# A channel-attention kernel on one core: the last row of two transfers sent in 16 narrow blocks

## The chip, the core and the metric

The kernel runs on one core of a Trainium2 chip. A core has five engines with a queue of instructions each: PE (TensorE, matrix products), DVE (VectorE), ACT (ScalarE), POOL (GpSimd) and SP (SyncE, which here does nothing but issue transfers). Transfers between the chip's memory (HBM) and the core's own memory (SBUF, 128 partitions) are carried out by 16 transfer engines, which the profile calls DMA engines. The metric is the time of one execution on the device in microseconds (us). Lower is better.

## The reference

```python
x: (1, 384, 384, 384) bfloat16      # batch, height, width, channels
g = einsum("bhwc->bc", x) / (H * W) # mean of each channel
s = sigmoid(g * w1d[0])             # k = 1: one weight, no neighbours
return x * s[:, None, None, :]
```

So there are 147,456 rows of 384 channels (768 bytes each). All of them have to be read before the first one can be scaled, and all of them are written.

## The kernel before

**Two passes.** The rows are spread over the 128 partitions, 1152 rows a partition. Pass one loads every row and adds it up; pass two multiplies every row by `s` and stores it. The SBUF tile `arena` has 275 rows a partition, far fewer than 1152, so pass one keeps only a part: 71 rows as they are, and 296 more packed four into three (`fold`, line 292, moves bits of every fourth row into spare bits of the other three; `unfold`, line 470, takes them out again). The other 785 rows of a partition are "streamed": they are read in pass one, summed and overwritten, and read a second time in pass two. That gives the 190.41 MB read and 113.25 MB written of the profile.

**The sum.** `sum_rows` (line 253) adds a row with one matmul against a tile of ones, into the PSUM tile `bank0`; each matmul (line 242) waits for the load of its row. `take_raw` (line 433) loads rows that stay as they are and sums them; the loop in line 437 ends pass one with slots of 13 rows and then V (8 rows), Y (8), T (5) and T+5 (3 rows). T and Y are scratch of `fold` and can be loaded only when the last `fold` is through. When the last row is summed, ACT computes the sigmoid (line 443) and copies it (line 447); then the scaling (line 456, mostly on DVE) and the stores (line 466) begin.

**Pass two** is laid out in advance by a small planner in Python (from line 564): it keeps a model time, decides which rows are scaled, unpacked, stored or loaded next, and so fixes the order of the instructions of each queue. It uses a cost for a row (`ROW`), for a load and for a store; nothing of it runs on the chip. The last store that it plans holds 15 rows a partition.

**Waits.** `Flow` (line 21) records every step with what it reads and writes. `Flow.emit` (line 68) turns the dependences into semaphore waits. Of a step's waits, all but one are put into the queue as wait instructions ahead of it (line 112), the last one rides on the instruction itself (line 117); the waits are sorted so that the latest step comes first (line 79). All loads and stores are issued by SP. The transfers use 24 semaphores in turn ("lanes", line 26), so a transfer also waits for the one 24 places before it. At the end SP waits for the last transfer of each lane (lines 123 and 124), in the order in which the lanes were first used.

Of the kernel before, what the change touches and what calls it, by code (L numbers as in the profile page):

```python
# [20 lines left out]
class Flow:  # L21
# [46 lines left out]
    def emit(self):  # L68
        nc = self.nc
        engines = {"SP": nc.sync, "ACT": nc.scalar, "PE": nc.tensor, "DVE": nc.vector, "POOL": nc.gpsimd}  # L70

        know = {e: {} for e in engines}

        def covers(k, d):
            return k.get(d.lane, 0) >= d.rank if d.dma else k.get(d.eng, -1) >= d.i

        for s in self.steps:
            k = know[s.eng]
            for d in sorted(s.deps, key=lambda d: -d.i):
                if covers(k, d):  # L80
                    continue
                s.waits.append(d)
                d.wanted = True
                for key, v in d.know.items():
                    if k.get(key, -1) < v:
                        k[key] = v
            s.know = dict(k)
            if s.dma:
                s.know[s.lane] = s.rank
            else:  # L90
                s.know[s.eng] = s.i

        count, sems = {}, {}
        for s in self.steps:
            if not s.dma and s.wanted:
                s.rank = count[s.eng] = count.get(s.eng, 0) + 1

        def sem(s):
            key = s.lane if s.dma else s.eng
            if key not in sems:  # L100
                name = f"f_{key[0]}{key[1]}" if s.dma else f"f_{key}"
                sems[key] = self.tc.alloc_semaphore(name)
            return sems[key]

        last = {}
        with self.tc.tile_critical():  # L106
            for s in self.steps:
                eng = engines[s.eng]
                waits = [(sem(d), d.rank * (16 if d.dma else 1)) for d in s.waits]
                hold = None if s.dma or not waits else waits.pop()  # L110
                for h, v in waits:
                    eng.wait_ge(h, v)  # L112
                ins = s.emit()
                if ins is None:
                    continue
                if hold:
                    ins = ins._wait_ge(*hold)
                if s.dma:
                    ins.then_inc(sem(s), 16)
                    last[s.lane] = s  # L120
                elif s.wanted:
                    ins.then_inc(sem(s), 1)
            for lane, s in last.items():
                engines[lane[0]].wait_ge(sem(s), 16 * s.rank)
# [3 lines left out]
def kernel(  # L128
# [11 lines left out]
    nc = tc.nc  # L140
    P = nc.NUM_PARTITIONS
# [4 lines left out]
    RPP = HW // P  # L146
# [15 lines left out]
    T = A + N_A  # L162
# [20 lines left out]
    ones = pool.tile([P, P], bf16, name="ones")  # L183
# [4 lines left out]
    arena = pool.tile([P, ROWS, C], bf16, name="arena")  # L188
# [10 lines left out]
    xf = x.rearrange("b h w c -> (b h w) c")  # L199
    of = out.rearrange("b h w c -> (b h w) c")  # L200

    def view(t, r0, n):
        return t[r0 * P : (r0 + n) * P, :].rearrange("(p r) c -> p r c", r=n)

    def rows(lo, n):
        return [("a", r) for r in range(lo, lo + n)]
# [17 lines left out]
    def raw(a):  # L224

        return c_raw + (a - U if a < G0 else PAIR + a - V)


    summed = [0]

    def load(chunk, a, lo, hi):

        r0, n = chunk
        fl.add(
            "SP",
            lambda: nc.sync.dma_start(out=arena[:, a : a + hi - lo, :], in_=view(xf, r0, n)[:, lo:hi, :]),  # L236
            writes=rows(a, hi - lo), dma=True,
        )
# [14 lines left out]
    def sum_rows(a, n):  # L253
        def emit(i, first, last):
            if first:
                return nc.tensor.matmul(acc, lhsT=ones[:], rhs=arena[:, i, :], start=first, stop=last)  # L256
            return add_held(arena[:, i, :], last)

        for i in range(a, a + n):
            first, last = summed[0] == 0, summed[0] == RPP - 1  # L260
            fl.add(
                "PE", lambda i=i, f=first, l=last: emit(i, f, l),
                reads=[("a", i), "ones"], writes=["bank0"],
            )
            summed[0] += 1

# [163 lines left out]
            stream_all(where[1])  # L430
    assert streamed[0] == N_STREAM

    def take_raw(a, n):
        load(KEPT, a, raw(a), raw(a) + n)
        sum_rows(a, n)

    for a, n in S2 + [(U, 8)] + S3 + S1 + [(V, 8), (Y, 8), (T, 5), (T + 5, 3)]:
        take_raw(a, n)
    assert summed[0] == RPP

    fl.add(
# [9 lines left out]
    def scale(a, n, eng="DVE", s=s_bf, after=()):  # L451
# [7 lines left out]
            reads=rows(a, n) + ["s_bf" if s is s_bf else "bank0"], writes=rows(a, n), after=after,  # L459
        )  # L460

    def store(chunk, a, lo, hi):
        r0, n = chunk
        return fl.add(
            "SP",
            lambda: nc.sync.dma_start(out=view(of, r0, n)[:, lo:hi, :], in_=arena[:, a : a + hi - lo, :]),
            reads=rows(a, hi - lo), dma=True,
        )
# [219 lines left out]
    while True:  # L688

        if dve_at <= now:  # L690
            ahead = backlog()
            can = bool(turns)
            if not can and not alongside and (ahead >= PENDING or not landed):
                can = start_group()
            if landed and (ahead < PENDING or not can):
                chunk, a, lo, n, end = landed.popleft()
                scale(a, n, s=s_ps if alongside and now else s_bf)
                dve_at = now + TT(n)
                since = (a, lo) if since is None else since
                if end or ahead < MERGE:  # L700
                    b, first = since
                    send(chunk, b, first, lo + n, stored(b, lo + n - first))
                    since = None
            elif can:
                f, t, then = turns.popleft()
                f()
                dve_at = now + t
                if then:
                    then()
        if alongside and alongside[0][0] <= now:  # L710
            _, chunk, a, lo, n = alongside.popleft()
            store(chunk, a, lo, lo + n)
            moves.append([now + LAT, n * ROW + PER_STORE, stored(a, n)])
        while waiting and waiting[0][0] <= now:
            _, n, then, chunk, a, lo, known = waiting.popleft()
            known.append(store(chunk, a, lo, lo + n))
            moves.append([now + LAT, n * ROW + PER_STORE, then])
        if not asked and not line and not turns:
            verdict()
            asked = True  # L720
        if out_rows == total and not checked:
            checked = True
            fl.add("POOL", again, reads=["odd_i", "s_bf"], writes=rows(Y, N_OVER), after=written)
        while over and over[0][0] <= now:
            over.popleft()[1]()

        got = runs()
        if bank_at is None and len(line) <= total - BANKS_AT and got and max(got)[0] >= PS * 4 // 3:
            a = max(got)[1]
            for i in range(a, a + PS * 4 // 3):  # L730
                idle[i] = False
            back = arena[:, a : a + PS, :].rearrange("p r c -> p (r c)")
            for i, bk in enumerate(banks):
                lo, hi = i * BANK, min((i + 1) * BANK, PS * C)
                copy_bank(i, bk[:, 0 : hi - lo], back[:, lo:hi], [("bank", i)], rows(a, PS))
            bank_at = (a, now + 5.0)
            got = runs()

        if got and todo < N_STREAM:
            n, a = max(got)  # L740
            n = min(n, CAP, N_STREAM - todo)
            ahead = backlog()
            if n >= BIG or n == N_STREAM - todo or (ahead < LOW and n >= 8) or ahead < LAST:

                lo = N_STREAM - todo - n
                load(STREAMED, a, lo, lo + n)
                for i in range(a, a + n):
                    idle[i] = False
                parts = [(STREAMED, a + e, lo + e, f - e, f == n) for e, f in split(n, PART)]
                todo += n  # L750
                moves.append([now + LAT, n * ROW + PER_LOAD, lambda parts=parts: landed.extend(parts)])

        if moves and moves[0][0] <= now:
            moves[0][1] -= DT
            if moves[0][1] <= 0:
                over.append((now + SEEN, moves.popleft()[2]))
        else:
            stall += DT
        if not (alongside or moves or waiting or over or landed or line or turns) and todo == N_STREAM:
            break  # L760
        now += DT
    fl.stall, fl.total = stall, now

    nc.scalar.preload_act_table(ACTF.Sigmoid)  # L764
# [31 lines left out]
```

## Time and profile before

| | us |
|---|---|
| median of 3 timed runs | 722.16 |
| lowest and highest | 721.12, 722.69 |
| span of the profiled execution, first to last instruction | 719.6 |
| DVE busy | 494.0 |
| PE busy | 210.5 |
| ACT busy | 115.7 |

A timed run also holds what lies around the span. The profile's page shows 20,160 transfer packets of 303.67 MB on SP's queue. Its views give, for any stretch of the span, the busy time of each engine and the share of the 16 transfer engines that were busy; a share of 0.25 means four of the 16. The chain of waits is the work that ended last, followed back from the end: at each step to what released it. "L242" is line 242 of the kernel; `arena<-in_x_dram` is a load, `out_dram<-arena` a store; `PEld` stands for weight loads and for waits in TensorE's queue, a small `q` for an engine's sequencer (`SPq` issues transfers). The profiler's times are of one execution.

### The profile page before, as it was taken

How to read it: one execution, taken by the hardware profiler on the slowest of the kernel's cores; microseconds unless marked ns; L12 is line 12 of the kernel's file. 1: busy time of each engine (PE TensorE's matmuls, PEld its weight loads, DVE VectorE, ACT ScalarE, POOL GpSimd, SP SyncE). 2: the span in 40 equal slices, each digit the busy share in tenths (PEclk: the TensorE clock that was granted, in tenths of full speed). 3: DMA queues.
4: the chain of work that ended last, by engine and by line, in shares of the span. 5: the costliest groups of instructions: out<-in, count | busy, mean ns of one | idle time of the engine just before them, and what ended most of it. 6: DMA issues, size and time to landing. Idle time of an engine off the chain costs nothing.

```text
span 719.6 us, 2061 instructions
## 1 busy us (share of the span) xinstructions
PE 210.5 (29%) x1202; PEld 0.3 (0%) x3; DVE 494.0 (69%) x471; ACT 115.7 (16%) x93; POOL 10.6 (1%) x7
## 2 busy tenths in 40 slices
PE   4678689888887770000000000000000000000000
PEld 0000000000000000000000000000000000000000
DVE  4600004887999819988999998999998985095500
ACT  3600003665777610002000000000000000000000
POOL 0000000000000005000000000000000000000000
PEclk9999999999999995555555555555555555555555
DMA  9999999999999979999999999999999999999997
GB/s 381 431 441 428 426 430 432 438 434 429 422 427 427 429 324 369 422 394 423 429 432 437 426 431 445 427 428 439 432 427 442 427 436 430 437 435 426 437 438 318
DMA packets 20173, 303.79 MB, mean 422 GB/s; under 512 B 2242, under 2 KB 2242, under 8 KB 6082
## 3 DMA queue, kind: packets, MB, share of 16 engines
q1 hardware_dynamic: 20160, 303.67, 99.0%
q8 instruction: 4, 0.07, 0.0%
q14 instruction: 7, 0.06, 0.0%
q10 hardware_dynamic: 2, 0.00, 0.0%
HBM read 190.41 MB, written 113.25 MB: 422 GB/s over the span
## 4 chain that ended last, share of the span: by engine, by line
DMA 61%; DVE 21%; ACT 6%; PE 5%; another core or an unknown queue 1%; SPq 0%; issue 0%; DVEq 0%
DMA arena<-in_x_dram 40%; DMA out_dram<-arena 21%; DVE arena L456 14%; ACT arena L313 6%; PE bank L242 5%; DVE arena L276 5%; DVE arena L282 2%; SPq L236 0%; ACT s_bf L443 0%; SPq L791 0%; DVEq L112 0%; SPq L106 0%
## 5 line engine op out<-in xcount | busy, mean ns | idle before, releaser
L456 DVE TENSOR_TENSOR arena<-arena,s_bf 128x4608 bf16<-128x4608 bf16 (+8 forms) x97 | 228.8, 2390 | 68.2 <-DMA arena<-in_x_dram 52.3
L276 DVE TENSOR_SCALAR arena<-arena 128x1536 uint16<-128x1536 uint16 (+2 forms) x247 | 145.3, 633 | 111.8 <-DMA arena<-in_x_dram 102.0
L242 PE MATMUL bank<-arena,ones 128*128 128x384 bf16 x1151 | 202.1, 336 | 48.9 <-DMA arena<-in_x_dram 48.9
L313 ACT ACTIVATE arena<-arena 128x3072 uint16<-128x3072 uint16 (+1 forms) x38 | 102.4, 2696 | 142.3 <-DVE arena L276 142.3
L282 DVE TENSOR_TENSOR arena<-arena 128x1536 uint16<-128x1536 uint16 (+2 forms) x114 | 121.0, 1061 | 5.2 <-PE bank L242 2.7
L529 PE MATMUL bank<-odd,ones 128*128 128x1 bf16 x1 | 0.2, 188 | 322.7 <-DVE odd L524 322.7
L456 POOL TENSOR_TENSOR arena<-arena,s_bf 128x1536 bf16<-128x1536 bf16 (+1 forms) x3 | 10.4, 3484 | 268.9 <-ACT bank L447 268.9
L386 ACT COPY arena<-bank 128x512 uint32<-128x512 uint32 (+1 forms) x7 | 4.0, 571 | 58.4 <-DMA out_dram<-arena 58.2
L456 DVE TENSOR_TENSOR arena<-arena,bank 128x1536 bf16<-128x1536 bf16 (+2 forms) x7 | 11.3, 1688 | 0.0
L242 PE MATMUL bank<-zeros,ones 128*128 128x384 bf16 x48 | 8.3, 326 | 0.0
L313 ACT ACTIVATION_READ_ACCUMULATOR arena<-arena 128x1 f32 x38 | 7.1, 186 | 0.0
L386 ACT COPY bank<-arena 128x512 uint32<-128x512 uint32 (+1 forms) x7 | 3.6, 566 | 0.0
L443 ACT ACTIVATE s_bf<-bank,w_sc 128x384 bf16<-128x384 f32 x1 | 0.6, 581 | 14.5 <-PE bank L242 14.5
L256 PE MATMUL bank<-arena,ones 128*128 128x384 bf16 x1 | 0.5, 478 | 6.9 <-DMA arena<-in_x_dram 6.9
L764 ACT ACT_TABLE_LOAD x1 | 1.3, 1283 | 0.7 <-PEq L780 0.7
L343 DVE TENSOR_SCALAR w_sc<-bank 128x1 f32<-128x1 f32 x1 | 0.2, 159 | 1.1 <-PE bank L338 1.1
L333 DVE MEMSET ones<- 128x128 bf16 x1 | 0.2, 165 | 1.0 <-SPq L106 1.0
L338 PE MATMUL bank<-w_bf,ones 1*128 1x1 bf16 x1 | 0.2, 181 | 2.1 <-DMA w_bf<-in_w1d_dram 2.1
L529 PEld LDWEIGHTS bank<-odd,ones 128*128 128x128 bf16 x1 | 0.1, 106 | 581.7 <-DVE odd L524 581.7
L533 DVE CAST odd_i<-bank 128x1 int32<-128x1 f32 x1 | 0.2, 159 | 0.3 <-PE bank L529 0.3
L447 ACT COPY bank<-s_bf 128x192 uint32<-128x192 uint32 x1 | 0.3, 323 | 0.0
L519 DVE TENSOR_REDUCE worst<-seen 128x1 f32<-128x38 f32 x1 | 0.2, 184 | 0.0
(8 smaller groups left out, 0.9 us busy)
## 6 DMA issues: line engine op xcount, KB each, us to landing
arena<-in_x_dram SPq DMA_DIRECT2D x15, 4608.0 KB, 35.4
arena<-in_x_dram SPq DMA_DIRECT2D x21, 1248.0 KB, 13.5
out_dram<-arena SPq DMA_DIRECT2D x7, 3072.0 KB, 33.1
arena<-in_x_dram SPq DMA_DIRECT2D x6, 3072.0 KB, 26.5
out_dram<-arena SPq DMA_DIRECT2D x4, 4608.0 KB, 39.2
arena<-in_x_dram SPq DMA_DIRECT2D x6, 2304.0 KB, 18.2
arena<-in_x_dram SPq DMA_DIRECT2D x3, 4512.0 KB, 27.0
out_dram<-arena SPq DMA_DIRECT2D x10, 1248.0 KB, 12.0
```

Of the source, the lines that this page charges most:

```text
L242: return pe.add_instruction(mybir.InstMatmult(name=nc.get_next_instruction_name(), ins=[pe.lower_ap(rhs), pe.lower_ap(ones[:])], outs=[pe. ...
L256: return nc.tensor.matmul(acc, lhsT=ones[:], rhs=arena[:, i, :], start=first, stop=last)
L276: lambda: nc.vector.tensor_scalar(out=dst, in0=src, scalar1=s0, scalar2=s1, op0=op0, op1=op1),
L282: "DVE", lambda: nc.vector.tensor_tensor(out=dst, in0=a, in1=b, op=op), reads=reads, writes=writes
L313: lambda: nc.scalar.activation(out=y, in_=y, func=ACTF.Copy, accum_out=seen[:, 2 * k + i : 2 * k + i + 1]),
L333: fl.add("DVE", lambda: nc.vector.memset(ones[:], 1.0), writes=["ones"])
L386: "ACT", lambda: nc.scalar.copy(dst.bitcast(u32), src.bitcast(u32)), reads=reads, writes=writes
L443: lambda: nc.scalar.activation(out=s_bf[:], in_=acc, func=ACTF.Sigmoid, scale=w_sc[:, 0:1]),
L447: "ACT", lambda: nc.scalar.copy(s_ps.bitcast(u32), s_bf[:].bitcast(u32)), reads=["s_bf"], writes=["bank0"]
L456: lambda: vec.tensor_tensor(out=v, in0=v, in1=s[:, None, :].to_broadcast([P, n, C]), op=Op.mult),
L529: lambda: nc.tensor.matmul(votes, lhsT=ones[:], rhs=odd[:], start=True, stop=True),
L764: nc.scalar.preload_act_table(ACTF.Sigmoid)
```

## The change

Three things are changed.

- The last load of pass one, three rows a partition to T+5, now loads two rows a partition. The third row (128 partitions x 768 bytes) follows in 16 transfers of 8, 15, 14, ... 2, 1 partitions. They are issued one after the other by SP. The matmuls of T+5 and of the two rows behind it depend on all of them.
- The last store, 15 rows a partition, now stores 14. Its last row is stored in 16 transfers of the same sizes, at the end of SP's queue.
- The closing waits go in the order in which each lane was last used.

All in all SP issues 172 transfers instead of 140, and TensorE's queue has eight more wait instructions, with two semaphores each. The order of instructions on the other engines stays as it is.

```diff
                 if s.dma:
                     ins.then_inc(sem(s), 16)
+                    last.pop(s.lane, None)
                     last[s.lane] = s
...
-    summed = [0]
+    summed, blocked = [0], []
...
-                reads=[("a", i), "ones"], writes=["bank0"],
+                reads=[("a", i), "ones"] + blocked, writes=["bank0"],
...
-    def take_raw(a, n):
-        load(KEPT, a, raw(a), raw(a) + n)
+    BLOCKS = [8] + list(range(15, 0, -1))
+    def take_raw(a, n, blocks=()):
+        r0, m = KEPT
+        load(KEPT, a, raw(a), raw(a) + n - bool(blocks))
+        p, i = 0, raw(a) + n - 1
+        for q in blocks:
+            to, frm = arena[p : p + q, a + n - 1 : a + n, :], view(xf, r0, m)[p : p + q, i : i + 1, :]
+            fl.add("SP", lambda to=to, frm=frm: nc.sync.dma_start(out=to, in_=frm), writes=[("b", a + n - 1, p)], dma=True)
+            blocked.append(("b", a + n - 1, p))
+            p += q
         sum_rows(a, n)
...
-        take_raw(a, n)
+        take_raw(a, n, BLOCKS if a == T + 5 else ())
...
+    n_stored, tails = [0], []
     def store(chunk, a, lo, hi):
         r0, n = chunk
+        n_stored[0] += hi - lo
+        if n_stored[0] == RPP:
+            hi -= 1
+            p = 0
+            for q in BLOCKS:
+                to, frm = view(of, r0, n)[p : p + q, hi : hi + 1, :], arena[p : p + q, a + hi - lo : a + hi - lo + 1, :]
+                tails.append((lambda to=to, frm=frm: nc.sync.dma_start(out=to, in_=frm), rows(a + hi - lo, 1)))
+                p += q
...
+    for f, r in tails:
+        fl.add("SP", f, reads=r, dma=True)
```

More of the change, by code (lines that the diff above doesn't have):

```diff
@@ L431 @@
     assert streamed[0] == N_STREAM
-    def take_raw(a, n):
-        load(KEPT, a, raw(a), raw(a) + n)
+    BLOCKS = [8] + list(range(15, 0, -1))
+    assert sum(BLOCKS) == P
+    def take_raw(a, n, blocks=()):
[7 more added lines that the diff above has]
+            p += q
         sum_rows(a, n)
     for a, n in S2 + [(U, 8)] + S3 + S1 + [(V, 8), (Y, 8), (T, 5), (T + 5, 3)]:
-        take_raw(a, n)
+        take_raw(a, n, BLOCKS if a == T + 5 else ())
     assert summed[0] == RPP
```

## The prediction

> **What bounds the kernel now.** I read the page first (busy times, transfer rates, chain), then the chain near the end of pass one, then busy shares in short windows around the two edited places, then the issues on SyncE's queue.
>
> ```profile
> span 719.6 us, 2061 instructions
> PE 210.5 (29%) x1202; PEld 0.3 (0%) x3; DVE 494.0 (69%) x471; ACT 115.7 (16%) x93; POOL 10.6 (1%) x7
> ...
> q1 hardware_dynamic: 20160, 303.67, 99.0%
> ...
> DMA 61%; DVE 21%; ACT 6%; PE 5%; another core or an unknown queue 1%; SPq 0%; issue 0%; DVEq 0%
> ```
>
> The 16 transfer engines are busy for 99.0% of the span, no compute engine for more than 69%. The bytes stay as they are, so what can move is the time in which the transfer engines are not full. There are two such places, and the change edits both: the turn from pass one to pass two, and the very end. First the chain at the turn (start, us, what), then busy shares in short windows there: the stretch, its length, busy us and count of PE, PEld, DVE, ACT and POOL, the granted clock, the share of the 16 transfer engines, GB/s.
>
> ```profile
> 254.13 11.35 DMA arena<-in_x_dram
> 265.49 0.04 issue
> 265.53 2.77 PE bank L242 x16
> 268.30 0.02 issue
> 268.33 0.59 ACT s_bf L443
> ```
> ```profile
> 264.50:264.90 0.40, 0.40 (x5) 0.00 (x0) 0.00 (x0) 0.00 (x0) 0.00 (x0) 1.00 1.02 411
> ...
> 265.70:266.30 0.60, 0.60 (x5) 0.00 (x0) 0.00 (x0) 0.00 (x0) 0.00 (x0) 1.00 0.32 129
> 266.30:266.70 0.40, 0.40 (x5) 0.00 (x0) 0.00 (x0) 0.00 (x0) 0.00 (x0) 1.00 0.19 75
> 266.70:267.10 0.40, 0.40 (x4) 0.00 (x0) 0.00 (x0) 0.00 (x0) 0.00 (x0) 1.00 0.05 17
> 267.10:270.70 3.60, 1.19 (x8) 0.00 (x0) 1.76 (x3) 0.90 (x2) 1.36 (x1) 1.00 0.00 0
> ```
>
> The engines do not finish together. At 264.9 all are busy, around 266 a share of 0.32 (five of 16), at 267.1 none; then nothing moves until 270.7. But the chain does not run through the last load. It runs through the load of Y (265.49) and the 16 matmuls behind it: eight rows of Y, five of T, three of T+5. The same picture at the end:
>
> ```profile
> 714.00:714.70 0.70, 0.00 (x0) 0.00 (x0) 0.00 (x0) 0.00 (x0) 0.00 (x0) 0.50 0.97 411
> 714.70:715.00 0.30, 0.00 (x0) 0.00 (x0) 0.00 (x0) 0.00 (x0) 0.00 (x0) 0.50 0.55 230
> 715.00:715.50 0.50, 0.00 (x0) 0.00 (x0) 0.00 (x0) 0.00 (x0) 0.00 (x0) 0.50 0.49 207
> 715.50:716.00 0.50, 0.00 (x0) 0.00 (x0) 0.00 (x0) 0.00 (x0) 0.00 (x0) 0.50 0.33 138
> 716.00:717.10 1.10, 0.00 (x0) 0.00 (x0) 0.00 (x0) 0.00 (x0) 0.00 (x0) 0.50 0.25 105
> 717.10:717.50 0.40, 0.00 (x0) 0.00 (x0) 0.00 (x0) 0.00 (x0) 0.00 (x0) 0.50 0.01 0
> ```
>
> From 716.0 to 717.1 a share of 0.25, four engines, decides the end. Behind 714.7 the shares times their windows add up to 0.85 us (0.165 + 0.245 + 0.165 + 0.275), so the mean engine is done at 715.55 and the last at about 717.2: at most 1.7 us could be won here by perfect balance.
>
> **The change part by part.** What one row weighs: a row is 768 bytes a partition, and a 128-partition transfer gives each engine eight of them. The rate of all 16 with full queues:
>
> ```profile
> 690.00:700.00 10.00, 0.00 (x0) 0.00 (x0) 0.00 (x0) 0.00 (x0) 0.00 (x0) 0.50 1.01 436
> ```
>
> 436 / 16 = 27.2 GB/s an engine, 28 ns for a row, 0.23 us for eight. So cutting the last row out of the big transfer ends that transfer 0.23 us earlier on every engine, and the 16 blocks then give the 128 rows back unevenly. If a block puts at most one row on an engine, an engine gets between 0 and 16 of them: between -0.23 and 16 x 28 ns - 0.23 = +0.22 us. Each row is now followed by a completion of its own, which no row of this trace prices; I let a row cost 28 to 56 ns (nothing for the completion, or as much again), so the upper end is 16 x 56 ns - 0.23 = +0.67. The Trainium skill, "DMA: Bandwidth & Descriptors", section "Why a DMA increments its semaphore by 16 and not by 1", states that a transfer of k partitions, k under 16, runs on the k lowest-numbered engines. By that, engine 0 gets 16 rows and engine 15 none, and the sum would be near -0.2 if the four late engines are the highest-numbered and near +0.6 if they are the lowest; no view here numbers the late engines.
>
> *End of pass two.* The last big store shrinks from 15 rows to 14 and 16 block stores follow. Are they issued in time?
>
> ```profile
> 253.29 2.23 SPq L236 DMA_DIRECT2D arena<-in_x_dram  x5
> ```
> ```profile
> 663.98 18.02 SPq L466 DMA_DIRECT2D out_dram<-arena  x3
> ```
> ```profile
> L236 SPq DMA_DIRECT2D arena<-in_x_dram x81: 327/340/938, 1.0 to 619.0; - x81
> ```
>
> Five issues in a row take 2.23 us, 0.45 each; the dearest of 81 took 0.94. The last store is issued by 682.0; 16 more are out by 689 (697 at 0.94), and the engines have work until 714: hidden. Each also waits for the transfer 24 places earlier, landed long before. What stays is the data, -0.23 to +0.67. An even deal, eight rows an engine at 28 to 56 ns, gives 0 to +0.22; I take its middle, +0.1.
>
> *The closing waits* (L124) now go in the order of transfers. Before, five of the twelve wait instructions came after the last landing:
>
> ```profile
> L124 SPq EVENT_SEMAPHORE  x12: 17/28/28, 682.1 to 718.1; - x12
> ```
> ```profile
> L124 SPq EVENT_SEMAPHORE  x5: 28/28/28, 717.9 to 718.1; - x5
> ```
>
> They stand 0.05 us apart. If the last thing to land is the last block, these 0.25 us go. If it is the big store on an engine without blocks, the block waits (16 lanes, two to an instruction, eight instructions) still follow it: 0.4 against 0.25. Bounds -0.25 to +0.2; I take -0.1.
>
> *End of pass one.* The load of T+5 becomes two rows and 16 block loads follow on SyncE, whose next task is a store at 269.9, so only the blocks' own landing matters. When is T+5 needed?
>
> ```profile
> L242 PE MATMUL bank<-arena,ones 128*128 128x384 bf16 x1151 | 202.1, 336 | 48.9 <-DMA arena<-in_x_dram 48.9
> ```
>
> The 16 matmuls take 2.77 us, of which the last one's own duration is 0.34; the other 15 starts stand 0.162 apart, so the first row of T+5 comes up at 265.53 + 13 x 0.162 = 267.64.
>
> ```profile
> arena<-in_x_dram SPq DMA_DIRECT2D x1, 288.0 KB, 12.2
> ```
> ```profile
> 0.93 0.52 ACTq L332 DMA_DIRECT2D w_bf<-in_w1d_dram  x1
> ```
> ```profile
> 2.14 0.10 PEld L338 LDWEIGHTS bank<-w_bf,ones 1*128 1x128 bf16 x1 [2.14 <-DMA w_bf<-in_w1d_dram]
> ```
>
> (First the issue of the old last load: out at 255.1, landed 12.2 later, 267.3. Then the only tiny transfer of the kernel and what waited for it.) The old load has 0.3 us in hand: making it land earlier is worth nothing, because the chain comes from Y. Could the blocks be late? Issued 0.45 apart from 255.5, the last one starts at 262.3; the tiny transfer took 1.2 us from issue to use; so it could land at 263.5, if its engines were free, and they have the earlier loads to finish. So a block lands when its engine has drained: 267.3 - 0.23, plus up to 16 rows at 56 ns, 267.1 to 268.0.
>
> The first matmul of T+5 now waits for 17 transfers: 16 further waits, two to an instruction, eight wait instructions on TensorE's queue, the latest block asked first. Behind them stand only three matmuls, then ScalarE's sigmoid and everything of pass two. The nearest rows:
>
> ```profile
> L112 PEldq EVENT_SEMAPHORE  x2: 51/51/51, 1.3 to 9.1; - x2
> ```
>
> At 51 ns each, eight are 0.41 us; twice that is my upper end. They run in front of the matmul, partly while T's five matmuls (0.8 us) still occupy the array. If the late engines have few rows, all is satisfied by 267.1 and most waits were passed before: 0. If a late engine has all 16, 268.0 + 0.41 (0.8) - 267.64: +0.8 to +1.2. Between ends 0 and +1.2 I take +0.3, near the lower end, since an even deal gives 267.3 and a few waits.
>
> A shift at the turn moves everything after it, for no transfer covers 267.1 to 270.7. The sum: +0.3 + 0.1 - 0.1 = **+0.3 us**, bounds 0 - 0.23 - 0.25 = -0.5 to 1.2 + 0.67 + 0.2 = +2.1. On the profiled execution: 719.6 to 719.9. The timed median is 722.16, 2.6 above that span (the three runs 1.5 to 3.1); nothing in the change touches what lies around it, so 722.16 + 0.3 = 722.5.
>
> **The rivals.**
>
> *Each block costs its engine a round trip (slower).* If an engine takes up the next block only when the last one's completion is confirmed, the price is the time from last data to landing: share 0.00 after 267.1 but landed 267.3, 0.2 us for loads; data gone by 717.5, waits passed from 717.9, 0.4 for stores. Sixteen blocks on one engine: 3.2 us behind 264.9 to 266.9 gives 268.1 to 270.1, +0.5 to +2.5 at the turn; 6.4 behind 714.7 to 717.2 gives 721 to 723.6, +3.7 to +6.2 at the end. Together +4 to +9, middle 729. It decides from about 0.1 us a block on a late engine. Against it: pass two opens with separate stores of 384 KB, and the share stays at 1.01, so completions do not pause an engine at that grain; but there eight rows' worth and more lies between two completions, here one row.
>
> ```profile
> out_dram<-arena SPq DMA_DIRECT2D x6, 384.0 KB, 2.5
> ```
> ```profile
> 270.70:274.00 3.30, 0.00 (x0) 0.00 (x0) 3.30 (x4) 0.00 (x0) 3.30 (x2) 0.53 1.01 409
> ```
>
> The Trainium skill speaks for this rival: "DMA: Bandwidth & Descriptors", section "Rules for kernel authors", wants small transfers coalesced, since under 64 KB one pays mostly overhead; its fixed 2.0 us (given for the gpsimd path), paid 16 times in series, would be 32 us, an estimate from that page which the overlap in the row above contradicts.
>
> *Narrow transfers are dear to issue (slower).* The last block's landing passes 267.64 when 15 issues and 1.2 us no longer fit behind 255.5: from 0.73 us an issue. At 0.94 it is 255.5 + 14.1 + 1.2 = 270.8: +3.2, 725.5. For it: the tiny transfer's issue took 0.52, more than 0.45. Against: that is still below 0.73.
>
> *The deal is not one row an engine.* If a narrow transfer's rows stay on one engine, it gets 128 rows, 3.6 us: about +3 at either end, 728.
>
> *Pass two falls out more evenly (faster).* The late engines of the end carry a lag from earlier mixing of loads and stores; a shifted start could deal it anew. Perfect balance gives the 1.7 us above: 720.5. The ramp itself can give no more than 0.23, eight rows.
>
> **How the numbers follow.** Forecast 0.64 (of it 0.58 within 0.2%, 0.05 slower, 0.01 faster); round trip 0.12; dear issue 0.08; one engine 0.04; more even 0.12 (0.08 faster, 0.04 within). 0.2% is 1.44 us, about what a measurement of this kernel can tell from no change. Faster 0.08 + 0.01 = 0.09; same 0.58 + 0.04 = 0.62; slower 0.05 + 0.12 + 0.08 + 0.04 = 0.29. The forecast's own range is 721.6 to 724.3. The range for eight in ten goes down to 721.0, halfway to the even case, and up to 726.0, past the dear issue, and leaves out the round trip and the one-engine case, 0.16.
>
> **What would show it.** Right: the last matmul of pass one ends between 268.3 and 269.5, block issues stand about 0.45 apart, the share of the transfer engines falls to zero within 1 us of where it did, both times. Round trip: a long stretch at a share of 0.06 (one engine) after 267 and after 717. Dear issue: SyncE's block issues reach beyond 266. Wrong altogether: if either tail shortens by more than 0.5 us, or if the stretch between 271 and 714 changes by over 1 us.

## The result and the profile after

| | before | after |
|---|---|---|
| median of the timed runs, us | 722.16 | 726.14 |
| lowest and highest, us | 720.7, 723.31 | 724.69, 727.02 |
| span of the profiled execution, us | 719.6 | 723.6 |

The ratio is 1.0056 with a 95% interval of 1.0042 to 1.007: **slower by 4.0 us (3.0 to 5.1)**. The forecast was 722.5, the range ended at 726.0. The page after, the lines that answer to those of before:

```profile
span 723.6 us, 2101 instructions
PE 215.1 (30%) x1202; PEld 0.3 (0%) x3; DVE 493.9 (68%) x471; ACT 115.7 (16%) x93; POOL 10.6 (1%) x7
...
q1 hardware_dynamic: 20672, 303.67, 98.4%
...
DMA 62%; DVE 22%; PE 5%; ACT 2%; another core or an unknown queue 1%; SPq 1%; issue 0%; DVEq 0%
```

The same bytes, and the same engine time apart from PE, which is counted busy 4.6 us longer without an additional matmul. The share of the transfer engines fell from 99.0% to 98.4%: the loss is time in which they move nothing. The chain of waits at the turn shows where (start, us, what):

```profile
260.05 9.54 DMA arena<-in_x_dram
269.59 0.38 issue
269.97 1.13 PE bank L243 x3
271.10 0.02 issue
271.12 0.59 ACT s_bf L454
```

The chain no longer comes through Y. It comes through a block issued at 260.05, the one with 4 partitions, which landed at 269.59. Before, the sigmoid started at 268.33; now at 271.12, **2.79 us later**. TensorE's timeline shows the same hole (start, us, line, and in brackets the idle time before and what ended it):

```profile
265.57 2.27 PE L243 MATMUL bank<-arena,ones 128*128 128x384 bf16 x13 [0.24 <-DMA arena<-in_x_dram]
...
269.97 1.12 PE L243 MATMUL bank<-arena,ones 128*128 128x384 bf16 x3 [2.12 <-DMA arena<-in_x_dram]
```

So the matmuls of Y and T end at 267.84, and the three of T+5 then wait 2.12 us for a transfer. What were the transfer engines doing meanwhile? Busy shares of after (columns as in the prediction):

```profile
266.30:266.70 0.40, 0.40 (x4) 0.00 (x0) 0.00 (x0) 0.00 (x0) 0.00 (x0) 1.00 0.34 112
266.70:267.10 0.40, 0.40 (x5) 0.00 (x0) 0.00 (x0) 0.00 (x0) 0.00 (x0) 1.00 0.10 25
267.10:267.50 0.40, 0.40 (x4) 0.00 (x0) 0.00 (x0) 0.00 (x0) 0.00 (x0) 1.00 0.03 8
267.50:269.90 2.40, 0.34 (x3) 0.00 (x0) 0.00 (x0) 0.00 (x0) 0.00 (x0) 0.99 0.00 0
269.90:271.10 1.20, 1.12 (x3) 0.00 (x0) 0.00 (x0) 0.00 (x0) 0.00 (x0) 0.50 0.00 0
```

And the count of data packets in the fourth of these windows:

```profile
DMA packets 0, 0.00 MB, mean 0 GB/s; under 512 B 0, under 2 KB 0, under 8 KB 0
```

Nothing. All data had moved by 267.5, as in the forecast, and yet transfers went on landing for 2.1 us. The trace keeps each step by which an engine raises a transfer's semaphore. Here is the last step of each block (a transfer has landed when its last engine has raised the semaphore):

```
block (partitions)   8     15     14     13     12     11     10     9      8      7      6      5      4      3      2      1
pass one, issued     255.53 255.96 256.34 256.76 257.17 257.57 257.97 258.34 258.70 259.04 259.37 259.71 260.05 260.39 260.70 261.01
pass one, landed     267.41 267.60 267.78 267.96 268.14 268.32 268.49 268.68 268.87 269.05 269.23 269.41 269.59 268.66 268.83 268.24
the end, landed      719.30 720.06 720.23 720.40 720.58 720.76 720.94 721.11 720.75 720.93 721.12 721.29 721.48 719.81 719.52 719.70
```

Read the middle row: thirteen landings, from the first block of 8 to the block of 4, stand 0.18 us apart ((269.59 - 267.41) / 12 = 0.182), although the issues were 0.31 to 0.43 apart and had ended at 261.3, six us before the first landing. The blocks of 3, 2 and 1, issued after the block of 4, landed before it. That is the picture of a block with at most one row an engine, always on the lowest-numbered engines (the trace numbers no engine; what it shows is that the narrower blocks use a part of the wider ones' engines): the fourth engine takes part in the thirteen blocks of 4 and more partitions and was the last one here; the blocks of 3, 2 and 1 do not use it. The step counts agree: a block of 15 shows one step 0.5 us after its issue and 15 later ones. The Trainium skill, "DMA: Bandwidth & Descriptors", section "Why a DMA increments its semaphore by 16 and not by 1", states this deal and that the issuing side raises the semaphore at once by what the unused engines would add; both agree with the trace.

The trace also keeps a record of every packet. The last twelve block rows of pass one start 0.039 us apart, up to 267.23, each with a packet of 4 bytes beside it, the last at 267.26. So an engine takes up the next block without waiting until the last one has landed; it is the landings that come 0.18 us apart, and they outlast the packets by 2.3 us.

The end shows the same in little. The busy shares, then the closing waits after the last landing (count, duration in ns, first and last start):

```profile
718.60:719.20 0.60, 0.00 (x0) 0.00 (x0) 0.00 (x0) 0.00 (x0) 0.00 (x0) 0.50 0.22 86
719.20:719.80 0.60, 0.00 (x0) 0.00 (x0) 0.00 (x0) 0.00 (x0) 0.00 (x0) 0.50 0.07 19
719.80:720.30 0.50, 0.00 (x0) 0.00 (x0) 0.00 (x0) 0.00 (x0) 0.00 (x0) 0.50 0.00 0
720.30:721.50 1.20, 0.00 (x0) 0.00 (x0) 0.00 (x0) 0.00 (x0) 0.00 (x0) 0.50 0.00 0
```
```profile
L125 SPq EVENT_SEMAPHORE  x4: 27/28/28, 721.5 to 722.0; - x4
```

Data is gone by 719.8; the last landing is at 721.48. The last big store had landed at 719.89, so the blocks behind it took 1.59 us. By those landings and the spans the 4.0 us are, in this pair of profiles: 2.79 at the turn; 0.85 in the stretch from sigmoid to last landing (450.36 against 449.51); 0.34 behind the last landing (2.14 against 1.80).

### The profile page after: what moved, and what is told of

It reads as the page before. It is cut to its first block, busy times and chain, and to the rows that moved or that the text cites. A ratio compares the mean times of both kernels' runs of the same rounds, so it can differ in the third digit from the quotient of the medians.

```text
span 723.6 us, 2101 instructions
## 1 busy us (share of the span) xinstructions
PE 215.1 (30%) x1202; PEld 0.3 (0%) x3; DVE 493.9 (68%) x471; ACT 115.7 (16%) x93; POOL 10.6 (1%) x7
## 3 DMA queue, kind: packets, MB, share of 16 engines
q1 hardware_dynamic: 20672, 303.67, 98.4%
## 4 chain that ended last, share of the span: by engine, by line
DMA 62%; DVE 22%; PE 5%; ACT 2%; another core or an unknown queue 1%; SPq 1%; issue 0%; DVEq 0%
DMA arena<-in_x_dram 42%; DMA out_dram<-arena 20%; DVE arena L467 15%; PE bank L243 5%; DVE arena L277 4%; DVE arena L283 3%; ACT arena L314 2%; SPq L237 1%; SPq L443 1%; ACT s_bf L454 0%; DVEq L112 0%; SPq L814 0%; SPq L106 0%
## 5 line engine op out<-in xcount | busy, mean ns | idle before, releaser
L243 PE MATMUL bank<-arena,ones 128*128 128x384 bf16 x1151 | 206.6, 341 | 47.3 <-DMA arena<-in_x_dram 47.3
L257 PE MATMUL bank<-arena,ones 128*128 128x384 bf16 x1 | 0.5, 478 | 6.8 <-DMA arena<-in_x_dram 6.8
```

The source lines that it names most:

```text
L243: return pe.add_instruction(mybir.InstMatmult(name=nc.get_next_instruction_name(), ins=[pe.lower_ap(rhs), pe.lower_ap(ones[:])], outs=[pe. ...
```

## The experiments

The theory after this result: **on one transfer engine the completions of small transfers come one behind another, 0.18 us each, and the engine that takes part in the most blocks sets the end.** The rivals: the cut itself (a further transfer, its waits) costs; narrow issue is dear; the uneven deal and not the number of transfers costs; the late start of pass two costs more than its own lateness. Each experiment was run beside the kernel before on the same chip (medians 721.2 to 721.8); the differences follow from the ratio. Diffs are against the changed kernel unless said otherwise.

**The parts by themselves.** Blocks only in pass one, old order of the closing waits:

```diff
-                    last.pop(s.lane, None)
...
-        if n_stored[0] == RPP:
+        if False:
```

> Pass one has the 16 block loads; the last store is one transfer of 15 rows and the closing waits go in the old order, as before the change. Completion theory (on each transfer engine the completion of a narrow transfer lands about 0.175 us behind the one before it, though its data takes 0.04 us; what counts is how many of the 16 a late engine gets): the changed kernel's profile shows the sigmoid at 271.12 instead of 268.33, so +2.8 us at the turn and nothing after it: 722.2 + 2.8 = 725.0. Queue theory (the price is in the issue of 32 more transfers and in the waits, half of it at either place): +2.0, 724.2. Even-out theory (a shifted start of pass two costs or wins by itself): the stretch from the first store to the end differs from the old one by over 0.5 us.

Blocks only at the end, with the new order of waits:

```diff
-        take_raw(a, n, BLOCKS if a == T + 5 else ())
+        take_raw(a, n)
```

> Pass one as before; the last store is cut into 14 rows and 16 block stores, closing waits in the order of transfers. Completion theory: the late engine 3 has 13 blocks, 13 x 0.175 = 2.3 us behind a data end that is 0.23 earlier, less what the late engines lead or trail in this run: by the two profiles +0.85 for the last landing and +0.3 behind it, 723.3 in all; up to +2.3 if the latest engine is also the lowest. Queue theory: +2.0, 724.2.

Only the new order of waits (against the kernel before):

```diff
                     ins.then_inc(sem(s), 16)
+                    last.pop(s.lane, None)
                     last[s.lane] = s
```

> Only the order of the closing waits is changed; no blocks. All theories: between the last landing and the end one wait instruction is left of five, 0.2 to 0.25 us less: 722.0, within the noise of the timing, but to be seen in the profile behind 717.9.

| | median, us | ratio (95%) | difference, us |
|---|---|---|---|
| blocks in pass one | 725.56 | 1.0051 (1.0038 to 1.0065) | +3.7 (2.7 to 4.7) |
| blocks at the end | 723.33 | 1.0021 (1.0012 to 1.003) | +1.5 (0.9 to 2.2) |
| order of waits | 722.12 | 1.0002 (0.9992 to 1.0012) | +0.1 (-0.6 to 0.9) |

The loads carry most of it. Their chain at the turn is that of the whole change again (the landings stand 0.20 us apart in this profile, (269.38 - 267.37) / 10):

```profile
260.04 9.40 DMA arena<-in_x_dram
269.44 0.56 issue
270.00 0.66 PE bank L242 x3
...
270.68 0.59 ACT s_bf L453
```

The sigmoid is 2.35 us late, and behind the last landing this kernel spends 2.16 us against 1.80, since in the old order twelve lanes follow that of the last store. About 1 us of its 3.7 remains; the stretch from sigmoid to last landing was 450.67 here, and it was between 449.51 and 451.07 in the profiled executions of the six kernels that store as before (the last store uncut), so a surplus of that size cannot be assigned. The stores' +1.5 is matched by the landings: the last big store at 718.22, the thirteenth block at 719.34, against 717.84 for the last store of before. The order of waits takes 0.24 us off the time behind the last landing (1.56 against 1.80), which the timed runs do not resolve. Loads and stores together give 5.2, the whole change 4.0; the intervals overlap.

**The same cut with other blocks**, at both places:

```diff
-    BLOCKS = [8] + list(range(15, 0, -1))
+    BLOCKS = [128]      # then 4 * [32], 8 * [16], 16 * [8]
```

> The last row is cut off at both places, but goes in a single transfer of 128 partitions, eight rows and one completion an engine. Completion theory: one completion more on each engine, 0.0 to 0.2 us at each place, of which the turn has 0.3 in hand: 722.0 to 722.3. Theory that the cut itself costs (a row of 768 bytes, the dependence of three matmuls on one more transfer, two more transfers): most of the +4.0 stays, 725 to 726.

> The last row in 4 transfers of 32 partitions at both places: two rows and one completion of each transfer on every engine, an even deal. Completion theory: 4 x 0.175 = 0.7 us for the last landing in place of 0.23 us of data: 267.1 + 0.7 = 267.8 at the turn, +0.2 to +0.4 with the waits; +0.5 at the end; 722.7 to 723.1. Uneven-deal theory (the price comes from laying more rows on the low engines): 722.0 to 722.3, as with a single transfer.

> The last row in 8 transfers of 16 partitions at both places: one row and one completion of each on every engine, eight an engine, an even deal. Completion theory: 8 x 0.175 = 1.4 us behind 267.1, 268.5 at the turn, +0.9 to +1.4 with waits and a slower matmul clock; +1.2 at the end; together 724.2 to 724.8. Uneven-deal theory: 722.0 to 722.3.

> The last row in 16 transfers of 8 partitions at both places: 16 rows on each of eight engines, none on the other eight. Completion theory: 16 x 0.175 = 2.8 us on every one of the eight, late ones among them: 267.1 + 2.8 = 269.9 landed, +2.8 to +3.3 at the turn; 2.8 - 0.23 = +2.6 at the end if the latest engine is one of the eight; 726 to 728, no faster than the changed kernel. Queue theory: as the changed kernel, 726.1.

Blocks of 32 and 16 partitions use all 16 engines evenly, blocks of 8 only eight of them. To tell number from unevenness there is a fifth kernel, with blocks only in pass one: 16 of 16 partitions, each half a row (384 bytes a partition), so that every engine has the bytes of the eight even blocks in twice as many transfers.

```diff
-        for q in blocks:
-            to, frm = arena[p : p + q, a + n - 1 : a + n, :], view(xf, r0, m)[p : p + q, i : i + 1, :]
+        for h in (0, C // 2) if blocks else ():
+            for p in range(0, P, 16):
+                to = arena[p : p + 16, a + n - 1 : a + n, h : h + C // 2]
+                frm = view(xf, r0, m)[p : p + 16, i : i + 1, h : h + C // 2]
...
-        if n_stored[0] == RPP:
+        if False:
```

> Blocks in pass one only, closing waits in the order of transfers: the last row in 16 transfers of 16 partitions and half a row (384 bytes) each, so every engine gets the same bytes as with 8 transfers of a whole row, but 16 completions instead of 8. Completion theory: 16 x 0.175 = 2.8 us behind 267.1, last landing 269.9, the first of the three matmuls at 270.0 to 270.4 (with 8 transfers it was 268.85): +2.4 to +3.2, 724.2 to 725.0. Theory that the bytes or the even deal count: as with 8 transfers at the turn, +1.2, 723.0.

| blocks | on the late engine | last landing of pass one | first matmul of T+5 | difference of the time, us |
|---|---|---|---|---|
| 1 of 128 | 1 | 267.49 | 267.74 | +0.1 (-0.6 to 0.7) |
| 4 of 32 | 4 | 268.12 | 268.18 | +0.5 (-0.1 to 1.2) |
| 8 of 16 | 8 | 268.79 | 268.85 | +2.5 (1.4 to 3.5) |
| 8, 15 to 1 (after) | 13 | 269.59 | 269.97 | +4.0 (3.0 to 5.1) |
| 16 of 16, half rows, loads only | 16 | 270.16 | 270.22 | +4.0 (2.5 to 5.5) |
| 16 of 8 | 16 | 270.36 | 270.42 | +5.4 (3.7 to 7.1) |

The chain with one block:

```profile
265.59 0.04 issue
265.63 2.77 PE bank L243 x16
```

with eight even ones, and their busy share after 267.5:

```profile
258.89 9.90 DMA arena<-in_x_dram
268.79 0.06 issue
268.85 0.66 PE bank L243 x3
```
```profile
267.50:268.80 1.30, 0.46 (x3) 0.00 (x0) 0.00 (x0) 0.00 (x0) 0.00 (x0) 1.00 0.00 0
```

and with sixteen half rows on every engine:

```profile
262.53 7.63 DMA arena<-in_x_dram
270.16 0.06 issue
270.22 0.66 PE bank L243 x3
```

With one block of 128 the chain comes through Y and 16 matmuls as before, and the time is that of before: the cut itself, the further transfer and its wait cost nothing that these runs resolve. Then the landing moves with the number of transfers on the late engine: (268.79 - 268.12) / 4 = 0.17 from four to eight, (270.16 - 268.79) / 8 = 0.17 from eight to sixteen, the latter with the same bytes on the same engines. So the number counts, not the bytes and not the unevenness. Between one landing and the next lie 0.18 us with eight engines to a transfer ((270.36 - 267.62) / 15 in 16 of 8) as with sixteen ((270.16 - 267.43) / 15 with half rows), so the completions queue on each engine and not at a place that all engines share. The deal matters only because it puts thirteen blocks on one engine where an even deal of 128 rows needs eight. With equal blocks 0.06 us lie between landing and matmul, with the ramp 0.38 and 0.56.

**Is it the landing alone, or does the engine lose time?** Two experiments put other data around the completions. In the first the 16 block loads go ahead of the loads of Y, T and T+5, with new closing waits and the last store uncut, so that the completions have the 15 rows of these loads, 1.5 MB, to hide behind:

```diff
...
+        if a == Y:
+            send_blocks(T + 5, 3)      # the 16 blocks, as soon as row T+7 is free
+        if a == T + 5:
+            blocked.extend(ahead)
...
-        if n_stored[0] == RPP:
+        if False:
```

> Blocks in pass one only, closing waits in the order of transfers: the same 16 block loads of 8, 15, ... 1 partitions, issued ahead of the loads of Y, T and T+5 instead of behind them, so that 15 rows (3.4 us an engine) follow; the three matmuls still wait for all blocks. Completion theory, completions land beside other data: the 2.3 to 2.8 us of completions pass under the 3.4 us of data; Y's load comes later by the blocks' own data on a late engine, 13 x 0.04 = 0.5 us: +0.3 to +0.8 at the turn, 722.1 to 722.6. Completions that hold up the data behind them: +2.3 to +2.8, 724.5, as with blocks behind.

723.9 us, ratio 1.0038 (1.0027 to 1.005), +2.7 us: a miss for the view that the completions cost nothing beside other data. The chain runs through Y again, but Y is late:

```profile
260.02 7.33 DMA arena<-in_x_dram
267.34 0.04 issue
267.38 2.77 PE bank L243 x16
```

Y landed at 267.34, against 265.49 before: 1.85 later. The busy shares from 262, first of this kernel and then of the kernel before, tell why:

```profile
262.00:263.00 1.00, 0.98 (x7) 0.00 (x0) 0.00 (x0) 0.00 (x0) 0.00 (x0) 1.00 1.04 337
263.00:264.00 1.00, 1.00 (x8) 0.00 (x0) 0.00 (x0) 0.00 (x0) 0.00 (x0) 1.00 1.06 347
```
```profile
262.00:263.00 1.00, 1.00 (x8) 0.00 (x0) 0.00 (x0) 0.00 (x0) 0.00 (x0) 1.00 0.97 406
263.00:264.00 1.00, 1.00 (x8) 0.00 (x0) 0.00 (x0) 0.00 (x0) 0.00 (x0) 1.00 1.02 424
```

Y is issued later too, behind the blocks (260.02 against 254.13), but the engines had work all the while: they are counted fully busy both times. Yet they move 337 and 347 GB/s where they moved 406 and 424. The packet records show how: of 185 packets of eight rows from 261.0 on, 36 took more than 0.26 us, the longest 1.13, and the others 0.23 to 0.26, where all of them took 0.23 before; together 11.7 us of the 16 engines' time. So the small transfers hold up the data behind them as well: the engine's time is lost, not only the message of the end delayed. The measured +2.7 is what the second theory forecast (+2.3 to +2.8).

In the second, the last store stays whole and goes as eight transfers of 16 partitions with 15 rows each, so that 11.5 KB an engine lie between two completions (pass one as before, new order of waits):

```diff
-            hi -= 1
...
+            for p in range(0, P, 16):
+                to, frm = view(of, r0, n)[p : p + 16, lo:hi, :], arena[p : p + 16, a : a + hi - lo, :]
```

> Pass one as before, closing waits in the order of transfers; the whole last store of 15 rows goes in 8 transfers of 16 partitions, one packet of 15 rows (0.43 us) and one completion of each on every engine. Completion theory, completions land beside the next packet: 0.43 is longer than 0.175, so nothing is added: 722.0. Completion theory, added to the data: 8 x 0.175 = +1.4, 723.6. Theory that transfers of few partitions are dear as such: +1.2 as with eight transfers of one row.

723.49 us, ratio 1.0031 (1.0018 to 1.0045), +2.2 us (1.3 to 3.2): a miss for the version in which nothing is added; +1.4, a completion added to the data of each transfer, lies inside the interval. In the profiled execution (span 720.7) the last four of these transfers landed 0.43 us apart (717.87, 718.31, 718.74, 719.17), which is the time of 15 rows at 28 ns, 0.42, with nothing added for the completion. But between the fourth and the fifth lie 0.75 (717.12 to 717.87), between the first and the second 0.78. The packet records show that the surplus lies in the data: 35 of the 128 packets of 15 rows took more than 0.44 us, the longest 2.27, where none of the 128 packets of the same size in the kernel before took more than 0.43. All 128 together took 24.1 us longer than at 0.43 each, 0.19 us for each packet and its completion. So here the completions are paid too, on average at the same price, but inside the data packets that follow. Why they fall so unevenly on the packets, and why the eight timed runs fell into two groups of four (722.2 to 722.8 and 724.2 to 725.4), the runs do not show.

**The start of pass two.** Is a late sigmoid worth its own lateness? Without any blocks, with the new order of waits, the sigmoid is computed five times, one after the other, so that pass two starts 4 x 0.61 = 2.4 us late (against the kernel before):

```diff
-    fl.add(
-        "ACT",
-        lambda: nc.scalar.activation(out=s_bf[:], in_=acc, func=ACTF.Sigmoid, scale=w_sc[:, 0:1]),
...
+    for _ in range(5):
+        fl.add(
+            "ACT",
+            lambda: nc.scalar.activation(out=s_bf[:], in_=acc, func=ACTF.Sigmoid, scale=w_sc[:, 0:1]),
...
```

> The kernel before with the closing waits in the order of transfers, no blocks; the sigmoid is computed five times over, which changes no value and starts pass two 4 x 0.6 = 2.4 us later. With blocks in pass one only, the first store started 2.4 us later too, but the whole grew by 3.8 (2.7 to 4.7). If a late start is simply handed on: +2.4, 724.2. If a late start of pass two costs by itself (its code, loads and stores meet otherwise): +3.4 or more, 725.2.

724.19 us, ratio 1.0034 (1.0022 to 1.0046), +2.5 us (1.6 to 3.3): handed on one to one, as far as the interval tells; the +3.4 of a late start that costs by itself lies just above it. And the last of TensorE's 2.79 us, the three matmuls at a granted clock of 0.50: with twelve matmuls on zeros, which add nothing to the sum, ahead of those of T+5:

```diff
+        if blocks:
+            keep_warm(12)
         sum_rows(a, n)
```

> The changed kernel, with 12 matmuls of zeros (they add nothing to the sum) ahead of the three matmuls that wait for the blocks. In the changed kernel's profile these three ran at a granted clock of 0.50 and took 1.12 us instead of 0.65. If the idle 2.1 us in front of them is what took the clock away, the clock stays at 1.00 and the three take 0.65 us, the sigmoid starts 0.4 us earlier than with the blocks alone; if not, 1.1 us as before.

```profile
267.44 2.11 PE L243 MATMUL bank<-zeros,ones 128*128 128x384 bf16 x12
269.96 0.65 PE L243 MATMUL bank<-arena,ones 128*128 128x384 bf16 x3 [0.40 <-issue]
```

The first matmul of T+5 starts where it did (269.96), since it waits for a landing; the three take 0.65 instead of 1.12, at a granted clock of 1.00, and the sigmoid starts 0.48 earlier, at 270.64. The one time was 726.19, so no gain was seen; one run cannot tell 0.5 us. Nor does it show that the zeros kept the clock up, for in three other kernels it stayed at 1.00 after as long a hole without them (last section). No kernel of these beats the kernel before; with one block, or the order of waits alone, it is equal within 0.1%.

## Why the prediction was wrong

**The step that failed: "I let a row cost 28 to 56 ns (nothing for the completion, or as much again)".** A row with a completion of its own costs 0.18 us on its engine, over three times the upper end. It costs that at both places, for loads and stores, for 768 bytes and for 384. Most of the 4.0 us follows from it and from the next point; 0.47 us at the turn and the closing waits do not.

**"An even deal ... I take its middle" failed too.** The rule that the prediction named beside it, the lowest-numbered engines, is what the landings show, and the last landing came from an engine with 13 blocks. With the right price, an even deal of eight gives 268.79, and thirteen give 269.59; with the price of the prediction, sixteen would have given 268.0. So the price was the larger error, the deal the smaller one.

**The turn, +0.3 (bounds 0 to +1.2): measured +2.79.** Of it, the landing is 2.27 later than that of the old last load (269.59 against 267.32), of which the cover in hand takes 0.32. That cover (the first row of T+5 comes up at 267.64) was worked out rightly, and the landings bear it out: with one block (267.49) the three matmuls follow those of T without a gap, with four (268.12) the array is idle for 0.16 us before them. The waits on TensorE's queue come to 0.38 behind the landing; 0.41 was the estimate for all eight. The remaining 0.47 is the granted clock, 1.12 against 0.65 us for three matmuls. It was not in the prediction at all: an idle engine was counted as costing its idle time only. It need not be so in every execution: three other kernels with as long a hole kept a clock of 1.00. 1.95 + 0.38 + 0.47 = 2.80.

**The end, +0.1 (bounds -0.23 to +0.67): measured about +1.4**, the 1.59 us from the last big store's landing to the last block's, less the 0.23 by which the big store was shortened; 0.9 by the same reckoning in the kernel with stores alone. It is less than at the turn because the engine with thirteen blocks was not the latest at the end: its first block landed at 719.30, the latest at 720.06. The stretch as a whole grew by 0.85 only; it differs by up to 1.6 us between profiled executions with the same last store, so the rest is not assigned.

**The closing waits, -0.1: measured +0.34 in the profile of after, -0.24 in that of the order alone.** In the order of issue the block of 4 has three more blocks behind it, although they landed earlier, and four wait instructions still follow the last landing. These alone take 0.5 us, with a gap among them that no row explains.

**Dear issue** fell: 16 issues of the loads took 0.31 us each in the middle, those of the stores 0.54, all of them hidden (min, median and max in ns, first and last start):

```profile
L443 SPq DMA_DIRECT2D arena<-in_x_dram x16: 243/306/381, 255.5 to 261.0; - x16
```
```profile
L483 SPq DMA_DIRECT2D out_dram<-arena x16: 512/538/611, 684.4 to 693.1; - x16
```

**The round trip** was the right kind of rival: one completion behind another on the late engine, to be decided "from about 0.1 us a block". Its mechanism, an engine that "takes up the next block only when the last one's completion is confirmed", is not what the packets show: at the turn an engine sends the next row after 0.039 us. Its prices, 0.2 for a load and 0.4 for a store, were read from single transfers, from the last data to the landing; in a row a completion costs 0.18 at either place, and thirteen count, not sixteen. So its 4 to 9 us had the result at their lower end, 4.0, and the 729 was too high. The argument against it ("completions do not pause an engine at that grain") was right for the grain that it named and said nothing of the one in question; with one packet of 15 rows to a completion, the eight deep stores already show a loss. The chance of 0.12 was too small for a price that no row showed: the bounds should have run from 28 ns to the 0.2 us that the trace did show behind a load's last data.

**Two of the signs were chosen badly.** "The share of the transfer engines falls to zero within 1 us of where it did" came true at the turn, 267.5 against 267.1; at the end it was 719.8 against 717.5, with a pass two that had started 2.79 later. "A long stretch at a share of 0.06" did not come, though completions were what held up the chain. They show as a share of 0.00 with a wait open. "The last matmul of pass one ends between 268.3 and 269.5" was the sign that worked: it ended at 271.1.

**The Trainium skill** spoke to the price in the page that the prediction named: "DMA: Bandwidth & Descriptors", section "Anatomy of one DMA — SWDGE (gpsimd) path", calls the semaphore write itself nearly free and puts the fixed cost into the confirmation that the last byte has arrived. The trace agrees that a transfer's end lags its data; that a further completion is nearly free it does not show, here it is 0.18 us each on an engine. These transfers go through SyncE's queue, not the path of that section.

What stays open: whether the confirmation of the data or the semaphore's write takes the 0.18 us (sending the next block does not, by the packets); why the loss with eight deep stores is so uneven; and the 1 us above the turn with loads alone.

## What to carry to other kernels

Price a small transfer by its completion on the engine that ends last, not by its bytes: here 0.18 us each against 0.028 for the 768 bytes, so a tail that is out of balance by a row or two an engine cannot be levelled with transfers of one row. Where a wait is open and the share of the transfer engines is 0.00, look for completions, and count how many transfers the latest engine takes part in. When an operation's price stands in no row, let the range reach to the nearest lag that a row does show, and compare the price with the gain (0.23 us at best here) before anything else.

## What the runs showed of the hardware

- Small transfers slow the data behind them: 337 to 347 GB/s at a full share, against 406 to 424 (blocks ahead of Y). A delayed packet is counted as busy: packets of eight rows took up to 1.13 us there instead of 0.23, packets of 15 rows up to 2.27 instead of 0.43 (eight deep stores).
- The granted clock fell to 0.50 after 2.12 us without a matmul in the profile of after, and stayed at 1.00 after 2.16, 2.39 and 2.36 us in three other kernels (loads only, 16 of 8, half rows). The Trainium skill, "TensorE: Matmul & The Clock Gate", section "Part 1: The HAM clock gate (the "warmup" mystery)", has the gate watch a free-running window of about 3.4 us; that the same idle time ended differently from one execution to the next agrees with a free-running window; that 2.12 us of idle time, less than one window, was enough in one of them does not agree with the one idle window that it asks for.
- An issue of a narrow load was no dearer than one of 128 partitions: 0.24 to 0.38 us each, in the main shorter with fewer partitions, where the loads just ahead of them took 0.43. That does not hold for the stores: the block stores took 0.51 to 0.61, and 0.73 to 0.91 with the stores alone, where the big store ahead of them took 0.33 and the one block of 128 partitions 0.64.
